# RWKV-7 attention and a four-expert mixture in one kernel: raw R loaded first, raw loads begun ahead of the x placement, later order of work from the seventh unit on

## The chip, the cores and the metric

The kernel runs on one core of one Trainium2 chip. The metric is the device time of one execution in microseconds (us). Before the change it is 1277.89 us, the median of 3 runs that lie between 1271.62 and 1294.58 us. The profiled execution took 1285.56 us, and its span from first to last instruction is 1283.8 us.

The engines are named as the profile names them: PE is TensorE (PEld its weight loads), DVE is VectorE, ACT is ScalarE, POOL is GpSimd, SP is SyncE, which here only issues transfers.

## The reference, cut to what matters

Two blocks follow each other. The first is a recurrence over 768 tokens, for 4 batches of 8 heads with 40 channels:

```python
for t in range(S):
    y[:, :, t] = np.einsum('bhd,bhde->bhe', rt, state)
    Sa = np.einsum('bhde,bhe->bhd', state, at)
    state = state * wt[:, :, None, :] - np.einsum('bhd,bhe->bhde', Sa, bt) \
            + np.einsum('bhd,bhe->bhde', vt, kt)
```

Its output, 3072 tokens by 320 channels, is the input x of the second block, a mixture of four experts with 1024 hidden channels each:

```python
for e in range(E):
    h = np.maximum(x @ w1[e], 0.0)
    out += p[:, e:e + 1] * (h @ w2[e])
```

Everything is float32.

## The kernel before, in words

**Units.** The recurrence is cut into chunks of 64 tokens. A *unit* is one chunk of two batches, so that its 128 tokens fill the partitions; there are 24 units. All units of one pair of batches hang together through `state`; two successive units belong to different pairs.

**The work of one unit.** It is spread over three generators, and the main loop (L1016 on) advances those of three successive units in turns.

- `within` (L385) is what needs no state. It turns the decays W into running products G and their reciprocals rG, brings B, A, K, V, R into channel order (tiles NT, AT, KT, VT, RT, by `turn_raw`, a DVE transpose at L229), multiplies three of them by rG or G (L423), and then runs small matmuls on PE: `pc` (L374) from RT and VT, `pfe` from NT, AT and KT, `pev`.
- `substitute` (L521) inverts small triangular blocks. DVE prepares M (L526 to L545: copies, the transpose L529, then L541 and L545), and POOL runs a serial chain of 48 small products and sums on tile Z (L554, L567).
- `merge` (L573) starts with two DVE transposes, Qc out of Z (L578) and QTc out of Qc (L580), goes on with `pY` and `pQ` on PE and fills QT.
- `step` (L613) brings in the state: `prn`, `psat`, `pxr`, `pdy` on PE, SX, Y and the new state on DVE, and at its end it places Y into the tile xT of the mixture. From the third chunk on this placement is 12 transfers (L718), which wait for Y.

**The mixture.** For each chunk of both pairs of batches (256 tokens) `mixture_of_chunk` (L822) puts 16 pieces of work on a list: per expert two `up` halves (ph, L733 and L741, read by ACT as hs, L746), and two pieces `down_1` (product p431) and `down_2` (products p75 and p26), which belong to the expert before. `down_2` comes with `add_h`, five DVE additions a1, a7, a5, a2, a6 of 512 columns (L842). DVE also adds the products onto the output tiles osb (L757, L759). `mix` takes pieces off the list and emits them between the stages of the recurrence; a regular unit emits 8, that is two experts: up, p431, up, p75 and p26, and the same again.

The PSUM buffers of `ph` and of the products share one tag, `mm`, with three buffers, so an `up` can only start when DVE or ACT has read what lay in its two buffers.

**Transfers.** SP issues nearly all of them in one queue, in the order of the program. Each of the six raw tiles (`rawW`, `rawA`, `rawB`, `rawK`, `rawV`, `rawR`) has one buffer, and is loaded by four transfers (six for W). The loads of unit u+3 but for W are put on a list `later`, and `begin_later` issues some of them behind every piece of the mixture; the weights w1 come in pieces of 640 KB through two buffers (L288).

**The order of the instructions.** The program is recorded in the order of the main loop. Instructions under `keep_in_program_order` keep that order among themselves, such as Qc, QTc, M and the transfers of `later`. All others are set by a scheduler that estimates when their inputs are there. On the chip each engine works through its own list in the order so found. From the unit with index 3 on (`q.u > PADDED`), the instructions of `within` are not kept in order, so the places of NT, AT, KT, VT, RT and of `pc` in their queues are the scheduler's.

**The main loop.** A flag `early` (L1036) decides where in unit u the stages of `merge` and `step` of unit u+1 stand: for early units the first stage of `merge` (Qc, QTc) comes in the third part of the loop, for later units in the second part, ahead of the pieces of the mixture there. It is set for u below 5.

Of the kernel before, what the change touches and what calls it, by code (L numbers as in the profile page):

```python
# [15 lines left out]
def kernel(  # L16
# [159 lines left out]
    units = []  # L176

    def begin(u):
        q = Unit()
        q.u, q.c, q.bp = u, u // (B // 2), u % (B // 2)  # L180
        q.b = [2 * q.bp, 2 * q.bp + 1]
        q.start, q.end = q.c == 0, q.c == NC - 1
        q.n = {}
        units.append(q)
        return q

    def load(q, names):
        for x in names:
            q.n[x] = t = sb.tile([P, H, D], FP32, name=f"nat{x}", tag=f"nat{x}", bufs=2 if x == "V" else 1)
            for i, bb in enumerate(q.b):  # L190
                nc.sync.dma_start(
                    out=t[i * L:(i + 1) * L], in_=srcs[x][bb, :, q.c * L:(q.c + 1) * L, :].rearrange("h t e -> t h e"),
                )

    def load_raw(q, names):


        moves = []
        for x in names:
            q.n["raw" + x] = t = raw[x]()  # L200
            heads = srcs[x].rearrange("b h t e -> (b h) t e")[q.b[0] * H:(q.b[1] + 1) * H, q.c * L:(q.c + 1) * L, :]
            heads = heads.rearrange("n (x two) e -> x n (two e)", two=2)
            for r in range(2):
                hs = slice(r, 16, 2)
                for y, los, w_ in ((0, (0,), D + Q), (1, (0, D) if x == "W" else (0,), D - Q if x == "W" else 2 * D - Q)):
                    o = slice(64 * r + Q * y, 64 * r + Q * y + Q)
                    for lo in los:
                        cols = slice(Q * y + lo, Q * y + lo + w_)
                        moves.append(
                            lambda eng, out=t[o, :, lo:lo + w_], in_=heads[:, hs, cols]: eng.dma_start(out=out, in_=in_)  # L210
                        )
        return moves
# [10 lines left out]
    def go(moves, eng=None):  # L223
        for move in moves:
            move(eng or nc.sync)
# [347 lines left out]
    def merge(q):  # L573


        Qc = sb.tile([P, H, Q], FP32, name="Qc", tag="q", bufs=2)
        QTc = sb.tile([P, H, Q], FP32, name="QTc", tag="q", bufs=2)
        tc.keep_in_program_order(nc.vector.transpose(out=dealt(Qc[:]), in_=q.Z))  # L578
        tc.keep_in_program_order(
            nc.vector.transpose(  # L580
                out=QTc[:].rearrange("p h r -> p (h r)"), in_=Qc[:].rearrange("p h c -> p (h c)"),
            )
        )
        q.QT = QTs()
        for i in range(P // Q):
            ins = nc.gpsimd.tensor_copy(out=q.QT[quarter(i), :, quarter(i % 2)], in_=QTc[quarter(i)])  # L586
            tc.keep_in_program_order(ins)
        yield

        py = big("pY")  # L590
        for h in range(H):
            for i in (1, 3):
                nc.tensor.matmul(
                    out=py[quarter(i - 1), h * Q:(h + 1) * Q], lhsT=q.F[quarter(i), h, 0:Q],
                    rhs=QTc[quarter(i), h, :], start=True, stop=True,
                )
        Y = sb.tile([P, H, Q], FP32, name="Yq")
        for i in (0, 2):
            nc.scalar.copy(out=Y[quarter(i)].rearrange("p h t -> p (h t)"), in_=py[quarter(i), 0:H * Q])
        yield  # L600

        pq = big("pQ")
        for h in range(H):
            for i in (0, 2):
                nc.tensor.matmul(  # L605
                    out=pq[quarter(i), h * Q:(h + 1) * Q], lhsT=Qc[quarter(i), h, :],
                    rhs=Y[quarter(i), h, :], start=True, stop=True,
                )
        for i in (0, 2):
            nc.scalar.copy(out=q.QT[quarter(i), :, quarter(1)], in_=by(pq[quarter(i), 0:H * Q], Q))  # L610
        yield
# [157 lines left out]
    def mixture_of_unit(q):  # L769

        hs, at = {}, 2 * E * q.u

        def ups(e):
            hs[e] = [up(at + 2 * e + x, q.xT, P, P) for x in range(2)]
            used(at + 2 * e + 2)
            if q.u == 0 and e + 2 < E:
                load_w2(e + 2)

        def down(e):
            po = ps.tile([P, DM], FP32, name="po", tag="mm", bufs=3)  # L780
            for f in range(NF):
                nc.tensor.matmul(  # L782
                    out=po[:], lhsT=hs[e][f // HF][:, f % HF, 0:P], rhs=w2_sb[e][:, f, :],
                    start=(f == 0), stop=(f == NF - 1),
                )
            if e == 0:
                q.osb = outputs()
            add(q.osb[:], po[:], scale(q, e), e == 0)
            if e == E - 1:
                store(q, q.osb)  # L790

        todo.append(lambda: ups(0))
        for e in range(E):
            todo.append(lambda e=e: down(e))
            if e + 1 < E:
                todo.append(lambda e=e: ups(e + 1))
# [111 lines left out]
    todo, last, later = [], [], []  # L908

    def begin_later(n):  # L910
        for move in later[:n]:
            tc.keep_in_program_order(move(nc.sync))
        del later[:n]

    def mix(n):

        for piece in todo[:n]:
            piece()
            begin_later(3 if n > 1 else 6)
        del todo[:n]  # L920

    def run(gen, n=99):
        if gen is None:
            return
        for _ in range(n):
            if next(gen, gen) is gen:
                break
# [3 lines left out]
    def begin_step(u):  # L931
        q = units[u]
        if q.bp == 0:
            chunks_x[q.c] = sb.tile([P, 3, 2 * P], FP32, name="xT", tag="xT", bufs=2)
        q.xT = chunks_x[q.c][:, :, q.bp * P:(q.bp + 1) * P]
        return step(q, q.xT)
# [57 lines left out]
    load(units[3], "BKV")  # L994
    go(load_raw(units[3], "ABKVR"))
    mix(3)
    m, s = merge(units[1]), begin_step(1)
    run(m, 1)
    mix(1)
    run(m)  # L1000
    run(s, 2)
    run(ws[2], 2)
    mix(1)
    run(ws[2], 2)
    substitute(units[2], nc.gpsimd)
# [10 lines left out]
    for u in range(1, NU):  # L1016
        q = units[u]
        m = s_next = w = w_next = iter(())
        if u + 1 < NU:
            m, s_next = merge(units[u + 1]), begin_step(u + 1)  # L1020
            w_next = ws[u + 1]
        if u + 2 < NU:
            w = ws[u + 2]

        def gap(n, pieces=None):
            at = 4 * u + n
            run(sum_ops, sums_at.get(at, 0))
            mix((1 if at in sparse else 2) if pieces is None else pieces)

        run(w, 1)  # L1030
        run(w_next)
        run(s, 1)
        gap(0)


        early = u < 5  # L1036
        run(s, 1)
        run(w, 1)
        run(s)
        if u == 1:  # L1040
            mixture_of_unit(q)
        elif q.bp:
            mixture_of_chunk(units[u - 1:u + 1], chunks_x[q.c])
        begin_later(len(later))
        run(w, 1)
        if not early:
            run(m, 1)
        gap(1)

        if u + 3 < NU:  # L1050
            go(load_raw(begin(u + 3), "W"))
            load(units[u + 3], "BKV")
            later.extend(load_raw(units[u + 3], "BAKVR"))
        run(w, 1)
        if early:
            run(m, 1)
        else:
            run(s_next, 1)
            run(m, 1)
        gap(2)  # L1060

        if not early:
            run(m, 1)
        run(w, 1)
        if not early:
            run(s_next, 1)
        if u + 2 < NU:
            substitute(units[u + 2], nc.gpsimd)
        run(w, 1)
        if u + 3 < NU:  # L1070
            ws.append(within(units[u + 3]))
            run(ws[u + 3], 1)
        if early:
            run(m, 1)
            run(s_next, 1)
            run(m)
            gap(3, 1)
            run(s_next, 1)
            mix(0 if 4 * u + 3 in sparse else 1)
        else:  # L1080
            gap(3)
        s = s_next
# [31 lines left out]
```

## Time and profile before

| what | measured |
|---|---|
| time, median of 3 | 1277.89 us |
| span of the profile | 1283.8 us |
| PE busy | 1200.6 us, 94% |
| DVE busy | 829.7 us, 65% |
| POOL busy | 475.2 us, 37% |
| ACT busy | 331.1 us, 26% |
| mean granted TensorE clock | 0.887 |
| moved through HBM | 94 GB/s over the span |

The page gives, under 2, the busy share of each engine in 40 equal slices, and the clock that PE was granted in each of them:

```profile
PE   5889988999999999999989999999999999999998
...
DVE  7865576789656756676566666676666766644334
POOL 4024555464253351552524515425244253350000
PEclk7789987999797887997979899789797997899999
```

Each digit is a tenth. PE is busy nearly throughout, and the recurrence ends some 150 us before the end, where POOL falls to 0 and only the mixture is left. The row PEclk is to be read beside the row PE: where it shows 7 or 8, PE was busy and yet worked on a reduced clock for part of the slice. A line of the groups reads: source line, engine, operation, tiles written and read, shapes, count, then the busy time in us and the mean ns of one, then the idle time just before and what ended it.

### The profile page before, as it was taken

The page shows a single profiled execution, that of the slowest core. Times are in us where ns is not written, and L with a number is a line of the kernel's source. Part 1 is how long each engine was busy: PE and PEld are TensorE (multiplying, and loading weights), DVE is VectorE, ACT ScalarE, POOL GpSimd, SP SyncE. Part 2 cuts the span into 40 slices and gives each one's busy share as a digit, 9 for nine tenths or more (in the row PEclk, how much of TensorE's full clock was granted, in tenths as well). Part 3 has the DMA queues.
Part 4 walks back from the last instruction along what each step waited for, and adds up shares of the span by engine and source line. Part 5 has one row for each costly group of instructions (what it writes and reads, how often), then busy time and mean ns, then how long its engine had stood idle before and what let it go on. Part 6 is the DMA issues. An engine that isn't in the chain of part 4 may idle for free.

```text
span 1283.8 us, 38036 instructions
## 1 busy us (share of the span) xinstructions
PE 1200.6 (94%) x15828; PEld 1045.6 (81%) x15828; DVE 829.7 (65%) x1642; ACT 331.1 (26%) x844; POOL 475.2 (37%) x1226
## 2 busy tenths in 40 slices
PE   5889988999999999999989999999999999999998
PEld 4767766888788888888878888888888887888887
DVE  7865576789656756676566666676666766644334
ACT  2222333223223122232231322322213323122110
POOL 4024555464253351552524515425244253350000
PEclk7789987999797887997979899789797997899999
DMA  7657642445334424443343443442434334212221
GB/s 147 141 135 196 137 91 67 98 101 125 84 99 100 105 74 99 95 114 85 84 109 85 108 104 87 104 99 72 107 86 112 86 104 89 84 57 86 86 76 31
DMA packets 299491, 126.73 MB, mean 99 GB/s; under 512 B 244360, under 2 KB 272696, under 8 KB 299320
## 3 DMA queue, kind: packets, MB, share of 16 engines
q1 hardware_dynamic: 296312, 123.84, 40.5%
q8 instruction: 125, 2.05, 0.7%
q10 hardware_dynamic: 3008, 0.46, 0.2%
q14 instruction: 46, 0.38, 0.1%
HBM read 116.36 MB, written 3.93 MB: 94 GB/s over the span
## 4 chain that ended last, share of the span: by engine, by line
PE 75%; DVE 10%; SPq 7%; DMA 5%; issue 2%; ACT 1%; DVEq 0%; ACTq 0%
PE ph L741 25%; PE p L848 20%; PE ph L733 9%; SPq L718 3%; PE pfe L374 3%; PE pdy L374 2%; PE psat L374 2%; PE prn L374 2%; DMA w1p<-in_moe_w_dram 2%; PE po L782 2%; SPq L210 2%; PE pxr L374 2%; PE pQ L605 2%; DVE osb L759 2%; PE pc L374 1%
## 5 line engine op out<-in xcount | busy, mean ns | idle before, releaser
L741 PE MATMUL ph<-xT,w1p 128*128 128x256 f32 (+1 forms) x1520 | 370.1, 400 | 0.0
L741 PEld LDWEIGHTS ph<-xT,w1p 128*128 128x128 f32 x1520 | 293.3, 203 | 74.6 <-issue 26.3
L567 POOL TENSOR_TENSOR Z<-Z 128x31 f32<-128x31 f32 (+7 forms) x704 | 256.9, 365 | 55.2
L554 POOL TENSOR_TENSOR Z<-M,Z 128x62 f32<-128x62 f32 (+7 forms) x352 | 156.0, 443 | 294.9 <-DVE M L545 258.6
L842 DVE TENSOR_TENSOR a<-hs 128x512 f32<-128x512 f32 x220 | 152.5, 710 | 145.6 <-ACT hs L746 145.6
L746 ACT ACTIVATE hs<-ph 128x512 f32<-128x512 f32 (+1 forms) x208 | 117.2, 564 | 439.9 <-PE ph L741 439.6
L759 DVE SCALAR_TENSOR_TENSOR osb<-p,gate,osb 128x320 f32<-128x320 f32 (+1 forms) x243 | 108.1, 480 | 128.6 <-PE p L848 125.1
L848 PE MATMUL p<-sums,a 128*128 128x160 f32 x1056 | 164.8, 299 | 0.0
L586 POOL COPY QT<-QTc 32x256 f32<-32x256 f32 x96 | 40.1, 418 | 326.7 <-DVE QTc L580 309.1
L848 PEld LDWEIGHTS p<-sums,a 128*128 128x128 f32 x1056 | 152.9, 190 | 2.2
L733 PE MATMUL ph<-xT,w1p 64*128 64x256 f32 (+1 forms) x760 | 138.1, 442 | 0.6 <-ACT xT L710 0.6
L848 PE MATMUL p<-w,hs 128*128 128x160 f32 x704 | 104.2, 301 | 0.0
L848 PE MATMUL p<-w,a 128*128 128x160 f32 x704 | 102.8, 299 | 0.0
L848 PEld LDWEIGHTS p<-w,hs 128*128 128x128 f32 x704 | 100.8, 191 | 2.3
L848 PEld LDWEIGHTS p<-w,a 128*128 128x128 f32 x704 | 98.0, 190 | 0.0
L733 PEld LDWEIGHTS ph<-xT,w1p 64*128 64x128 f32 x760 | 79.5, 207 | 20.1 <-issue 6.3
L439 DVE RECIPROCAL rG<-G 128x504 f32<-128x504 f32 x24 | 79.1, 3296 | 0.0
L634 ACT COPY SN<-prn 64x256 f32<-64x256 f32 x88 | 32.2, 366 | 159.0 <-DVE EV L630 156.6
L529 DVE STREAM_TRANSPOSE M<-blocks 128x1024 f32<-128x1024 f32 x24 | 46.3, 1931 | 35.4 <-ACT blocks L526 35.1
L374 PE MATMUL pc<-RT,VT 40*64 40x64 f32 x768 | 21.2, 264 | 40.4 <-DVE RT L229 39.0
L374 PEld LDWEIGHTS pc<-RT,VT 40*64 40x64 f32 x768 | 17.3, 168 | 46.7 <-DVE RT L229 43.6
L374 PE MATMUL pdy<-VC,k_tok 64*64 64x104 f32 (+1 forms) x768 | 43.6, 269 | 0.0
(153 smaller groups left out, 1489.7 us busy)
## 6 DMA issues: line engine op xcount, KB each, us to landing
w1p<-in_moe_w_dram SPq DMA_DIRECT2D x95, 512.0 KB
w1p<-in_moe_w_dram SPq DMA_DIRECT2D x190, 64.0 KB
w<-in_moe_w_dram SPq DMA_DIRECT2D x4, 1280.0 KB
sums<-in_moe_w_dram SPq DMA_DIRECT2D x9, 512.0 KB
out_dram<-osb SPq DMA_DIRECT2D x46, 80.0 KB
rawW<-in_w_dram SPq DMA_DIRECT2D x47, 72.0 KB
natB<-in_b_dram SPq DMA_DIRECT2D x42, 80.0 KB
natK<-in_k_dram SPq DMA_DIRECT2D x42, 80.0 KB
```

The lines of the kernel that those rows point to most:

```text
L374: nc.tensor.matmul(out=p[row][half(col), lo + at * out_cols:lo + (at + 1) * out_cols], lhsT=lhsT, rhs=rhs, start=(n == 0), stop=(n == len( ...
L439: pin(nc.vector.reciprocal(out=rG[:, :, 0:L - 1], in_=Gv[:, :, 1:L]))
L529: ins = nc.vector.transpose(out=M[:], in_=cols)
L554: ins = eng.tensor_tensor(out=Z[:, 1:3, 0:n, j + 1:Q], in0=M[:, j:j + 2, None, j + 1:Q].to_broadcast([P, 2, n, m]), in1=Z[:, here, 0:n, j: ...
L567: eng.tensor_tensor(out=z[:, 0], in0=z[:, 0], in1=z[:, x], op=ALU.add)
L586: ins = nc.gpsimd.tensor_copy(out=q.QT[quarter(i), :, quarter(i % 2)], in_=QTc[quarter(i)])
L733: nc.tensor.matmul(out=ph[i][:, f, :], lhsT=w1.last[i * DT:(i + 1) * DT, f, :], rhs=xT[i * DT:(i + 1) * DT, 2, :], start=(f == 0), stop=False,
L741: nc.tensor.matmul(out=ph[i][:, f, :], lhsT=w1.main[:, g, at * P:(at + 1) * P], rhs=xT[:, g, :], start=False, stop=(g == 1 and f == HF // ...
L746: nc.scalar.activation(out=h[:, i * HF // 2:(i + 1) * HF // 2, 0:n], in_=ph[i][:], func=ACTF.Relu,)
L759: nc.vector.scalar_tensor_tensor(out=to, in0=p, scalar=sc, in1=to, op0=ALU.mult, op1=ALU.add)
L842: nc.vector.tensor_tensor(out=t[:], in0=x, in1=y, op=op)
L848: nc.tensor.matmul(out=p[:, n * HD:(n + 1) * HD], lhsT=a[:, f, :], rhs=b[:, f, :], start=(f == 0), stop=(f == HF - 1),)
```

## The change

It has four parts.

1. The list `later` is filled in the order R, B, A, K, V instead of B, A, K, V, R.
2. Behind each piece of the mixture four raw transfers are issued instead of three, where `mix` has more than one piece to emit.
3. What is left of the list is issued ahead of the last stages of `step`, and so ahead of the 12 transfers of the placement. It stood behind them before.
4. The flag `early` holds for u below 6 instead of 5, so the later order of the loop begins at the seventh unit.

It is meant to have RT in time for `pc`, and to keep raw loads from standing behind transfers that wait for Y.

```diff
@@ def mix(n)
         for piece in todo[:n]:
             piece()
-            begin_later(3 if n > 1 else 6)
+            begin_later(4 if n > 1 else 6)
@@ for u in range(1, NU)
-        early = u < 5
+        early = u < 6
         run(s, 1)
         run(w, 1)
+        begin_later(len(later))
         run(s)
         if u == 1:
             mixture_of_unit(q)
         elif q.bp:
             mixture_of_chunk(units[u - 1:u + 1], chunks_x[q.c])
-        begin_later(len(later))
         run(w, 1)
@@
             load(units[u + 3], "BKV")
-            later.extend(load_raw(units[u + 3], "BAKVR"))
+            later.extend(load_raw(units[u + 3], "RBAKV"))
```

## The prediction

> **What bounds the kernel now.** The page gives PE 94% busy, so I asked for PE's waits first. One row stands out:
>
> ```profile
> PE pc L374 <- DVE RT L229: 39.0, 18, 3.2
> ```
>
> Columns: total us, times, longest. From 334 us on it is 16 times the same 2.16 us, once a unit. The timeline of PE, then of DVE, around two of them, and SP and POOL between:
>
> ```profile
> 490.29 1.25 PE L848 MATMUL p<-sums,a 128*128 128x160 f32 x8
> 493.70 0.69 PE L374 MATMUL pc<-RT,VT 40*64 40x64 f32 x32 [2.16 <-DVE RT L229]
> ```
>
> ```profile
> 485.21 2.35 SPq L210 DMA_DIRECT2D rawR<-in_r_dram  x2
> ```
>
> ```profile
> 439.88 0.58 DVE L578 STREAM_TRANSPOSE Qc<-Z 128x256 f32<-128x256 f32 x1
> ...
> 456.71 0.69 DVE L545 TENSOR_TENSOR M<-M,Z 128x512 f32<-128x512 f32 x1
> ...
> 492.64 0.38 DVE L759 SCALAR_TENSOR_TENSOR osb<-p,minus_gate,osb 128x160 f32<-128x160 f32 x1
> 492.94 0.70 DVE L229 STREAM_TRANSPOSE RT<-rawR 128x512 f32<-128x512 f32 x1
> 493.56 0.58 DVE L578 STREAM_TRANSPOSE Qc<-Z 128x256 f32<-128x256 f32 x1
> ```
>
> ```profile
> 457.55 0.29 POOL L554 TENSOR_TENSOR Z<-M,Z 128x62 f32<-128x62 f32 x1 [14.30 <-DVE M L545]
> ...
> 479.66 0.51 POOL L567 TENSOR_TENSOR Z<-Z 128x8 f32<-128x8 f32 x2
> 494.76 1.29 POOL L586 COPY QT<-QTc 32x256 f32<-32x256 f32 x3 [14.58 <-DVE QTc L580]
> ```
>
> The raw R was asked for at 485-487.6, and RT ran at 492.94 directly behind osb additions: the wait is the DVE queue, not a late transfer. The second thing to see is POOL: from M (457.40) to the end of the chain (480.2) it needs 22.7 us, and Qc, which reads its result, stands in DVE's queue only at 493.56, 13 us later. This chain costs nothing today.
>
> The windows show what the wait does beyond its 2.16 us (PE, PEld, DVE, ACT, POOL busy, then the granted clock):
>
> ```profile
> 438.00:440.00 2.00, 0.00 (x0) 0.00 (x0) 2.00 (x5) 0.00 (x0) 0.00 (x0) 1.00 0.34 49
> ...
> 442.00:444.00 2.00, 2.00 (x66) 1.82 (x62) 1.06 (x4) 0.73 (x2) 1.15 (x3) 0.50 0.68 118
> ...
> 458.00:460.00 2.00, 2.00 (x16) 1.97 (x15) 0.00 (x0) 0.60 (x1) 1.56 (x6) 1.00 0.10 23
> ```
>
> ```profile
> 440.01:493.70 53.69, 51.53 (x661) 44.94 (x661) 34.48 (x68) 13.71 (x35) 20.90 (x53) 0.84 0.38 90
> 493.70:545.76 52.06, 49.90 (x660) 43.56 (x660) 34.66 (x68) 13.71 (x35) 20.54 (x53) 0.87 0.42 99
> 545.76:593.71 47.95, 45.43 (x661) 40.39 (x661) 34.55 (x68) 13.71 (x35) 21.07 (x53) 0.96 0.43 102
> ```
>
> After each wait the clock is halved, for 17.1, 13.7 or 3.4 us. Units of equal work take 53.7, 52.1 and 47.95 us accordingly, 52.1 on average (334.33 to 1115.52 is 15 units). Taking the wait and the rest of the halving out leaves 47.95 - 2.16 - 1.4 = 44.4 us.
>
> **What the Trainium skill says.** "Perfetto Trace Analysis", section Tensor Engine Instruction, says ACT, DVE and GpSimd are strict FIFO: a waiting DVE instruction holds all behind it. The trace agrees: RT, with its data there, waited for its place. "TensorE: Matmul & The Clock Gate", Part 1, says an idle window of about 3.4 us puts PE on half clock, a busy one restores it. The lengths found are multiples of 3.4 us, but here 2.16 us idle was enough, and the measurement decides. "GPSIMD Engine Reference", section 1, says POOL shares its SBUF interface with DVE: L554 on 128x152 ranges up to 1006 ns, beside a median of 398 for the line, and the chain took 20.25 us at 90-110 us, 21.5 in the last unit, 22.7 otherwise.
>
> **The change part by part.** No operation is added or removed; every count stays.
>
> Loads (R first, four behind a piece, the rest ahead of the placement): SP issues the same transfers. The two rawR transfers behind the placement (2.35 us) move ahead of it, where SP stood waiting for Y (472.5 to 476.26). PE has no waits on w1p rows, so this is worth 0 by itself.
>
> What it moves is the scheduled order, and that I read from the built programs, for index 8 on. On PE `pc` moves ahead of p75 and p26, or between them. On DVE, RT moves from the end of the unit to right behind SX, and Qc, which in both programs follows RT closely, moves with it. Before, 45 DVE instructions stand between M (L545) and the Qc that reads its chain. After, in 10 units only 7 to 14 (adds of p431, SX, RT, then Qc: "near"), and in 6 units 21 (also a1, a7, a5, a2 and p75's adds: "far"). The POOL order is unchanged. So DVE will reach Qc long before POOL is done and stand there, with additions, Y, AT, KT, VT queued behind. PE soon follows: its third `up` needs the PSUM buffer that p75's adds free (near), or p431 the one p26's adds free (far). A loop forms that was hidden: M, POOL chain, Qc, the DVE and PE work to the next M.
>
> Its length I walk at full clock. Durations are from the rows of the unit at 440-494: up 4.6 us (474.43 to 479.05), p431 3.35 (to 482.40), up 4.6 (to 487.03), p75 with p26 4.4; DVE and ACT rows are the ones shown in the same timeline (a 0.68, an add of 320 columns 0.5, of 160 columns 0.3).
>
> - Near. Qc 0.58, QTc 0.45, a1 and a7 1.36, p75's adds and a5 1.5: the third up may start 3.9 us after Qc began. PE then does up 4.6, p431 3.35, up 4.6 and p75 2.2, so pc comes at 18.7. VT is there by then (DVE has some 14 us of work, and one a1 that waits for the last up). Then pc 0.55, prn 1.0, pY 0.55, p26 2.2, pQ 0.55, pfe 0.95, psat 0.9: 25.4. ACT's SaT, SX and blocks (2.65; 451.07 to 453.63) have to pass before DVE's transpose L529: 28.1. L529 to L545 take 3.4: M is ready 31.6 after Qc.
> - Far. p75's adds stand ahead of Qc, so PE is held only at p431, until p26's adds and a6 are done: 2.1. p431 and up end at 10.1. But VT comes behind QTc 0.45, NT 0.65, Y and state 3.7, rG on NT 0.7, AT 1.35, four adds 1.6, KT 1.35 and its own 0.65, together 10.4 of DVE: 12.5. So pc at 12.6 with a wait of 2.4 before it; then the same small products with p75 and p26, 8.9; ACT 2.65; and DVE has the 3.3 us reciprocal (L439) between L529 and L545. M is ready 31.3 after Qc.
>
> To both comes POOL's chain. With DVE mostly idle beside it, it is unknown between the shortest seen, 20.25, and the usual 22.7; I take 20.5 (near) and 21 (far), since the two short ones were those with the least DVE work beside them. With 0.15 from M to POOL the loops are 52.3 and 52.4 us.
>
> The idle PE costs clock as well. Ahead of a near Qc, PE runs out of work at 42.5 (far loop: psat 21.5, up, p431, 1.5 for pev and pxr, up, 4.4, 2.5 for pdy and pg) and is freed at 52.4 + 3.9: nearly 14 us idle. Ahead of a far Qc it runs out at 50.9 and is freed at about 54.5: some 4 us. Both exceed 2.16 us, so the clock halves every time. Dense up work then needs one or two windows of 3.4 us to restore it: 3.4 to 6.8 us at half speed, on average a loss of 2.5 us, which I add to the near loop; in the far loop VT's 12.5 hides it. Near 54.8, far 52.4.
>
> Sum: from the first early Qc (index 8) to the last (23) are 10 near and 5 far loops: 810 us, now 1115.38 - 387.82 = 727.6. That is +82. The first comes earlier: M at about 345 (now 351.73) plus 20.5 is 366 instead of 387.8: -22. Behind the last Qc are now 168.4 us; after, pc follows at 12.6, and from pc on 168.3, less 5.5 us of halved clock, plus 4.4 for p75 and p26: 179.8, +11. In all +72: 1350 us.
>
> `early` below 6 concerns one unit, whose Qc stays behind pc; taken as 0 beside the 6 us above.
>
> **The rivals.**
>
> - The wait goes and the clock stays full: 15 units at 44.4 instead of 52.1, and 7 in the last: -123, 1155 us. For it: RT and VT stand early enough for pc. Against: POOL's 22.7 us after M would have to fit ahead of Qc; it overruns by over 10.
> - DVE stalls, but the halved clock falls on idle time: 785 us of loops, 1325.
> - Nothing measurable: a chain below 19 us and more PE overlap give loops of 50, 750 us: 1290. Against: no chain below 20 in the trace.
> - Worse: chain at 22.7 and two more windows at half clock, near 59.5, far 56.7: 879 us, 1419.
>
> **How the numbers follow.** Forecast 0.50, milder stall 0.24, worse 0.12, faster 0.07, nothing measurable 0.07. The range 1305 to 1400 takes in forecast, the milder stall and the lower half of the worse case. Faster 0.07, same 0.08, slower 0.85.
>
> **What would show it.** Right: DVE waits on POOL Z at L578, 8 to 15 us each, 16 times; PE waits of several us at ph L733 and p L848 on DVE osb; the row pc <- RT gone; loops from Qc to Qc of 52 to 55 us; POOL chains nearer 20 than 22.7. Wrong: no such DVE wait, or PE going on while DVE stands, which would need PSUM buffers free that I count as taken.

## Result and the profile after

The changed kernel takes 1340.42 us (median of 3 runs, 1337.48 to 1342.32) against 1277.89. The ratio is 1.0512, with a 95% interval from 1.0436 to 1.0589: slower by some 5%. This ratio and those of the experiments leave slow runs out (here the one of 1294.58 us), and the experiments are compared with runs of the kernel before made beside them (medians 1282.63 and 1284.18 us), so the ratios differ a little from the quotients with 1277.89.

PE's waits after, with the columns as before (total us, times, longest). The row `pc <- RT` is gone, and PE now stands before `up`, with a smaller new wait of `pg` for rG:

```profile
PE ph L733 <- issue: 106.0, 11, 12.3
PE pg L341 <- DVE rG L440: 23.9, 8, 4.0
...
PE pc L374 <- DVE VT L229: 7.9, 3, 3.7
```

"issue" says only that the view saw no releaser. DVE's waits give the reason. The row of Qc before, then after:

```profile
DVE Qc L578 <- POOL Z L567: 3.5, 1, 3.5
```

```profile
DVE Qc L578 <- POOL Z L567: 162.8, 17, 16.7
```

Before, Qc waited once, in the last unit. Now it waits for POOL's chain 17 times. One of these waits, on DVE, POOL and PE, in the timelines (start us, duration us, engine, line, operation, then the idle time before it in brackets):

```profile
647.05 0.69 DVE L545 TENSOR_TENSOR M<-M,Z 128x512 f32<-128x512 f32 x1
647.66 1.59 DVE L759 SCALAR_TENSOR_TENSOR osb<-p,gate,osb 128x320 f32<-128x320 f32 x4
649.16 0.77 DVE L381 COPY_PREDICATED SX<-mask_up,pxr 128x256 f32<-128x256 int32 x2
649.82 0.71 DVE L229 STREAM_TRANSPOSE RT<-rawR 128x512 f32<-128x512 f32 x1
666.95 0.61 DVE L578 STREAM_TRANSPOSE Qc<-Z 128x256 f32<-128x256 f32 x1 [16.42 <-POOL Z L567]
```

```profile
647.89 0.29 POOL L554 TENSOR_TENSOR Z<-M,Z 128x62 f32<-128x62 f32 x1 [28.05 <-DVE M L545]
...
666.40 0.51 POOL L567 TENSOR_TENSOR Z<-Z 128x8 f32<-128x8 f32 x2
```

```profile
648.30 3.72 PE L741 MATMUL ph<-xT,w1p 128*128 128x256 f32 x16
...
658.63 0.70 PE L733 MATMUL ph<-xT,w1p 64*128 64x256 f32 x2
671.06 2.04 PE L733 MATMUL ph<-xT,w1p 64*128 64x256 f32 x6 [11.74 <-issue]
673.04 5.03 PE L741 MATMUL ph<-xT,w1p 128*128 128x256 f32 x16
```

RT runs right behind SX, and Qc is next in DVE's queue, 16.4 us before POOL is done (666.91). All of DVE's work stands behind it, among it the osb additions that free PSUM. PE runs dry at 659.3 and starts again 4.1 us after Qc. The last line shows what the idle time costs on top: the same 16 matmuls that took 3.72 us at full clock take 5.03.

Where the 56.6 us between the two spans (1283.8 and 1340.4) lie, cut at the start of the first Qc that moved ahead and of the last one before the last unit (the 8th and the 23rd):

| stretch | before | after | difference |
|---|---|---|---|
| start to the 8th Qc | 334.2 | 327.0 | -7.2 |
| 8th to 23rd Qc, 15 loops | 781.2 | 834.1 | +52.9 |
| 23rd Qc to the end | 168.4 | 179.3 | +10.9 |

### The profile page after: what moved, and what is told of

It is laid out like the page before. It is cut to its first block, busy times and chain, and to the rows that moved or that the text cites. A ratio compares the mean times of both kernels' runs of the same rounds, so it can differ in the third digit from the quotient of the medians.

```text
span 1340.4 us, 37990 instructions
## 1 busy us (share of the span) xinstructions
PE 1152.9 (86%) x15828; PEld 1001.3 (75%) x15828; DVE 818.2 (61%) x1642; ACT 330.8 (25%) x844; POOL 451.8 (34%) x1226
## 4 chain that ended last, share of the span: by engine, by line
PE 62%; DVE 15%; issue 8%; POOL 5%; DMA 3%; SPq 3%; ACT 3%; DVEq 0%; ACTq 0%; POOLq 0%
PE ph L741 22%; PE p L848 18%; PE ph L733 7%; POOL Z L567 3%; PE pdy L374 3%; PE po L782 3%; DVE rG L439 2%; SPq L718 2%; POOL Z L554 2%; DVE M L529 2%; DMA w1p<-in_moe_w_dram 2%; DVE osb L759 2%; PE psat L374 1%; PE pfe L374 1%; DVE G L402 1%
## 5 line engine op out<-in xcount | busy, mean ns | idle before, releaser
L554 POOL TENSOR_TENSOR Z<-M,Z 128x62 f32<-128x62 f32 (+7 forms) x352 | 138.4, 393 | 555.6 <-DVE M L545 446.7
L567 POOL TENSOR_TENSOR Z<-Z 128x31 f32<-128x31 f32 (+7 forms) x704 | 235.1, 334 | 55.2
L733 PE MATMUL ph<-xT,w1p 64*128 64x256 f32 (+1 forms) x760 | 131.1, 444 | 106.6 <-issue 106.0
L733 PEld LDWEIGHTS ph<-xT,w1p 64*128 64x128 f32 x760 | 77.9, 210 | 129.3 <-issue 117.3
L848 PE MATMUL p<-sums,a 128*128 128x160 f32 x1056 | 165.7, 300 | 0.0
L848 PEld LDWEIGHTS p<-sums,a 128*128 128x128 f32 x1056 | 152.2, 190 | 2.1
L578 DVE STREAM_TRANSPOSE Qc<-Z 128x256 f32<-128x256 f32 x24 | 14.8, 618 | 162.8 <-POOL Z L567 162.8
L848 PE MATMUL p<-w,hs 128*128 128x160 f32 x704 | 104.7, 302 | 0.0
L848 PE MATMUL p<-w,a 128*128 128x160 f32 x704 | 104.7, 300 | 0.0
L848 PEld LDWEIGHTS p<-w,hs 128*128 128x128 f32 x704 | 101.4, 192 | 2.2
L586 POOL COPY QT<-QTc 32x256 f32<-32x256 f32 x96 | 52.6, 548 | 147.7 <-DVE QTc L580 142.6
L848 PEld LDWEIGHTS p<-w,a 128*128 128x128 f32 x704 | 98.2, 190 | 0.3
L374 PE MATMUL pdy<-VC,k_tok 64*64 64x104 f32 (+1 forms) x768 | 48.0, 274 | 0.0
L374 PE MATMUL pdy<-SX,n_tok 64*64 64x104 f32 (+1 forms) x768 | 46.3, 264 | 0.4 <-DVE SX L381 0.4
```

The costliest lines, as they stand in the source:

```text
L374: nc.tensor.matmul(out=p[row][half(col), lo + at * out_cols:lo + (at + 1) * out_cols], lhsT=lhsT, rhs=rhs, start=(n == 0), stop=(n == len( ...
L554: ins = eng.tensor_tensor(out=Z[:, 1:3, 0:n, j + 1:Q], in0=M[:, j:j + 2, None, j + 1:Q].to_broadcast([P, 2, n, m]), in1=Z[:, here, 0:n, j: ...
L567: eng.tensor_tensor(out=z[:, 0], in0=z[:, 0], in1=z[:, x], op=ALU.add)
L733: nc.tensor.matmul(out=ph[i][:, f, :], lhsT=w1.last[i * DT:(i + 1) * DT, f, :], rhs=xT[i * DT:(i + 1) * DT, 2, :], start=(f == 0), stop=False,
L848: nc.tensor.matmul(out=p[:, n * HD:(n + 1) * HD], lhsT=a[:, f, :], rhs=b[:, f, :], start=(f == 0), stop=(f == HF - 1),)
```

## The experiments

Two theories. **Stall:** R first lets RT float up to SX, and Qc goes with it (its instruction is tied behind the one recorded just before it on DVE, which is RT; in the trace after, Qc follows RT directly or 4 instructions later in every unit from the 8th to the 23rd), so DVE waits for POOL; without that the change would have gained, since it takes away the wait of `pc`. **Transfers:** the raw loads, issued earlier, set the time by when they land or by what they collide with.

### Each part alone

R first, nothing else:

```diff
-            later.extend(load_raw(units[u + 3], "BAKVR"))
+            later.extend(load_raw(units[u + 3], "RBAKV"))
```

> The kernel before with only the order of the raw loads changed (R, B, A, K, V); three behind a piece, the rest behind the placement, early below 5. In its built DVE order 7 instructions stand between M and Qc in 16 units. Stall theory (R first moves RT, and Qc behind it, so that DVE stands at Qc for POOL): all loops are of the near kind, 57 us, so 16 waits of DVE on POOL Z of 12 to 17 us and a time of 1340 to 1390 us, no better than the full change. Transfer theory (what costs is the larger share of raw loads issued early, ahead of w1 pieces and placement, and R first is harmless): within 2% of the kernel before, 1255 to 1300 us.

Measured: 1448.83 us, ratio 1.1236 (1.1147 to 1.1325). Its waits of PE and of DVE:

```profile
PE ph L733 <- issue: 132.7, 18, 11.0
PE pc L374 <- DVE VT L229: 39.6, 18, 3.2
```

```profile
DVE Qc L578 <- POOL Z L567: 236.2, 18, 16.5
```

The direction is that of the stall, and the size goes beyond what was expected of it. The second row gives a reason: here `pc` still stands behind p26 in PE's queue and now waits for VT, the last of the five, 39.6 us in place of the 39.0 for RT. The old wait was kept and the stall added, in every unit from the 7th to the 23rd, with Qc 7 or 8 instructions behind M, near, from the 8th on. The loops are 60.6 us on average, (1249.1 - 339.4)/15, where 57 was expected.

The other three parts without R first:

```diff
-            begin_later(3 if n > 1 else 6)
+            begin_later(4 if n > 1 else 6)
...
-        early = u < 5
+        early = u < 6
...
+        begin_later(len(later))
         run(s)
...
-        begin_later(len(later))
```

> The changed kernel with the raw loads in the old order B, A, K, V, R; the other three parts stay. Qc stands 33 to 44 DVE instructions behind M. Stall theory: no wait at Qc of more than 2 us, pc already ahead of p75 and p26 on PE and so without its 2.16 us wait in most units; units of 45 to 49 us, time 1165 to 1230 us. Transfer theory: the loss stays, 1320 to 1350 us. A third view, that the later order of work costs: 1300 to 1350 us.

Measured: 1203.09 us, ratio 0.9351 (0.9295 to 0.9408). The wait of `pc` fell to 6.1 us, and Qc waits for POOL twice, 7.5 us in all. So one line of the change turns a gain of 6.5% into a loss of 5.1%. Which of the three brings the gain, the next three runs tell, each with one of these hunks alone.

> Of the change only part 2 is done: four raw transfers behind a piece of the mixture instead of three. In the built program pc then stands behind the second up or behind p75 and no longer behind p26, RT stands behind VT and ahead of the osb additions of p26, and 31 to 44 DVE instructions lie between M and Qc, so Qc has POOL's chain done when it is reached. Theory (the wait before pc and the clock that it halves are what before loses; DVE's stall at Qc is what the change loses): the pc <- RT row falls from 39 us to below 10, no wait on POOL Z at Qc, time 1190 to 1225. Rival (the gain of the version with all parts but R comes from the raw loads ahead of the placement or from the later order): 1260 to 1295, as before.

Measured: 1212.96 us, ratio 0.9444 (0.9383 to 0.9505).

> Of the change only part 3 is done: what is left of the raw loads is issued ahead of the placement. In the built program pc stays behind p26 as before; in every second unit RT stands behind a6 and all additions of osb, in the others as before; 41 to 52 DVE instructions lie between M and Qc. Theory (a load that starts earlier is worth nothing where the wait is DVE's queue): the pc <- RT row keeps its size, 30 to 45 us, no stall at Qc, time 1255 to 1300. Rival (the wait before pc is a late transfer of raw R, as the edit's purpose says): the row falls below 10 us and the time to 1190 to 1225.

Measured: 1279.88 us, ratio 1.0023 (0.9997 to 1.0049).

> Of the change only part 4 is done: the later order of the loop begins one unit later. In the built program only the units around it differ, from index 10 on 45 DVE instructions lie between M and Qc and RT is behind the additions of p26, as before. Theory (it concerns one unit): 1265 to 1290, pc <- RT at 35 to 45 us. Rival (it sets the order of all later units and so carries the gain): below 1230.

Measured: 1280.61 us, ratio 0.9963 (0.9922 to 1.0004).

The row of `pc` in the waits of these three, in the same order:

```profile
PE pc L374 <- DVE RT L229: 6.1, 2, 3.2
```

```profile
PE pc L374 <- DVE RT L229: 48.4, 17, 3.7
```

```profile
PE pc L374 <- DVE RT L229: 36.8, 17, 3.2
```

Four transfers behind each piece is the part that gains, and it gains by order: `pc` moves ahead of p26, and RT ahead of the additions that waited for it. Raw loads ahead of the placement, the part meant to have R there in time, leave the row at 48.4 us. No trace lists a wait of RT for its transfer either. This refutes the late transfer as the cause of the wait before `pc`: it was DVE's queue. That the loads ahead of the placement leave the time as it was hides a trade, more idle time at a higher clock: `pQ` waits 25.2 us for ACT there, where it was 2.2, and the mean clock is 0.902 in place of 0.887.

### Qc moved back, all else kept

In the changed kernel RT is recorded ahead of VT, so that Qc is tied behind VT. PE's order and that of the transfers on SP stay as in the changed kernel from first to last; DVE's differs (`PADDED` is 3; the kernel keeps the order of `within` for `q.u <= PADDED`, so its places are the scheduler's from the unit with index 4 on, not 3):

```diff
+            if q.u >= PADDED:
+                q.RT = by_channels("RT", "RT", 2, "R")
             VT = by_channels("VT", "turned", 3, "V")
-            q.RT = by_channels("RT", "RT", 2, "R")
+            if q.u < PADDED:
+                q.RT = by_channels("RT", "RT", 2, "R")
```

> The changed kernel with all four parts; only RT and VT are recorded in the other order, R before V, so that Qc is kept behind VT instead of behind RT. PE's order stays that of the changed kernel. Stall theory: waits at Qc fall from 163 us to under 25 us, the PE waits at ph go with them, units of 45 to 49 us, time 1165 to 1230 us. If the loss comes from RT or the loads instead: 1320 to 1350 us.

Measured: 1201.63 us, ratio 0.9339 (0.9266 to 0.9412), with every load where the change has it. DVE waits at Qc twice, and PE before `up` (L736 in this kernel) twice, 2.1 us in all. DVE's row, and what stays of PE's rows above:

```profile
DVE Qc L581 <- POOL Z L570: 6.0, 2, 5.2
```

```profile
PE pg L341 <- DVE rG L443: 23.5, 7, 4.0
...
PE pc L374 <- DVE VT L229: 6.9, 2, 3.7
```

This is the decisive run. The kernels of 1340 and of 1202 us issue the same transfers and the same matmuls in the same order; the place of Qc, 0.6 us, and of what is tied to it in DVE's queue makes the difference of 139 us. It also beats both kernels.

### Half the chain

The changed kernel with the second half of POOL's substitution left out (8 of its 16 steps are done):

```diff
-        for j in range(0, Q, 2):
+        for j in range(0, Q if at_once else Q // 2, 2):
```

> The changed kernel with the second half of POOL's chain left out (8 of the 16 steps of the substitution on POOL, so the inverted blocks are incomplete); order of DVE and PE as in the changed kernel. Stall theory: the chain takes 9 to 11 us instead of 19 to 21, each near loop falls by about 10 us until PE's 44 to 46 us of work hold, time 1180 to 1230 us, waits at Qc still there but under 8 us each. If POOL's chain isn't what holds the loop: within 2% of the changed kernel, 1315 to 1365 us.

Measured: 1233.02 us, ratio 0.9595 (0.953 to 0.9661). DVE's row:

```profile
DVE Qc L578 <- POOL Z L567: 56.1, 9, 7.1
```

A chain of 9.8 us in place of 19.2 gives back 107 us of the changed kernel's 1340, and the wait of a near Qc falls from 16.4 to 7.1, by as much as the chain is shorter. POOL's chain is thus what DVE waits for. The gain is shared out otherwise than expected: the loops behind a near Qc fell from 57.7 to 52.1 us and not by 10, those behind a far Qc from 51.3 to 43.4, since from the 13th Qc on the chain that a near Qc waits for runs in these. Even the half is too long for the near place, and the version with the whole chain and Qc behind VT is faster than this one.

### How long an idle time halves the clock

The kernel with Qc behind VT keeps 7 waits of `pg` of up to 4.0 us: it needs the reciprocal of 8 columns (0.20 us), which stood behind four additions (1.5 us) that stood behind the reciprocal of 504 columns (3.3 us). The order of the two is turned and the long one tied behind the short:

```diff
-        pin(nc.vector.reciprocal(out=rG[:, :, 0:L - 1], in_=Gv[:, :, 1:L]))
         pin(nc.vector.reciprocal(out=rG[:, :, L - 1:L], in_=q.gl[:]))
+        pin(nc.vector.reciprocal(out=rG[:, :, 0:L - 1], in_=Gv[:, :, 1:L]), True)
```

> The changed kernel with RT recorded ahead of VT, as in the run of that edit, and in addition the reciprocal of 8 columns (0.2 us) recorded ahead of that of 504 columns (3.3 us), which is pinned behind it. In that earlier run pg waited 7 times for the small reciprocal, which stood behind four additions of osb (1.5 us): 23.5 us in all, up to 4.0 us each, and the clock was halved for 3.4 to 6.8 us behind each. Theory (the idle time itself halves the clock, and 2.2 us are enough): the waits shrink to some 2.5 us each, 15 to 18 us in all, the clock is still halved behind each, and the time falls by 5 to 12 us from 1202 only, 1188 to 1200. Rival (only an idle time near 3.4 us or more halves the clock): behind waits of 2.5 us the clock stays full, and the time falls by 20 to 30 us, 1170 to 1185. Second rival (these waits are hidden): 1200 to 1206.

Measured: 1200.68 us, ratio 0.9354 (0.9296 to 0.9412). That cannot be told from 0.9339 without it; the row fell to 16.3 us and a new one, pdy behind SX, has 7.1. The time lies at the edge of the second rival's range, and as a way to gain time the edit failed. For the clock it is worth more, because one wait became far shorter than the others. Two of its waits on PE's timeline, and windows behind them (the columns end with clock, DMA share, GB/s):

```profile
538.70 0.93 PE L341 MATMUL pg<-ident,rG 128*128 128x128 f32 x4 [2.65 <-DVE rG L443]
```

```profile
820.83 0.63 PE L341 MATMUL pg<-ident,rG 128*128 128x128 f32 x4 [0.85 <-DVE rG L443]
```

```profile
540.00:543.00 3.00, 2.63 (x11) 1.56 (x11) 0.64 (x2) 1.47 (x4) 2.53 (x7) 0.50 0.06 11
...
821.50:824.50 3.00, 2.00 (x13) 1.45 (x14) 1.27 (x5) 1.47 (x4) 2.45 (x8) 1.00 0.26 49
```

The first window lies behind the wait of 2.65 us and has half the clock; behind 0.85 us the clock stays full. All five waits of 2.59 to 2.67 us from 536 us on were followed by 3.4 to 6.8 us of halved clock, the one of 0.85 us by none. Behind three of the five, though, a second wait of 1.0 us (`pdy`) came before the clock fell; only two, at 538.70 and 634.34, stand alone, beside the 16 of 2.16 us in the kernel before. So an idle time well below 3.4 us can be enough, and the expectation that only one near 3.4 us does it is refuted.

The length of one wait does not decide it, though. In the run with R first alone, `pc` waits 2.16 us in 16 units, and behind 5 of these waits the clock stays full. Two of the 16 end at 426.91 and 488.66 us. The windows around each (behind the span stands PE's busy time):

```profile
423.51:426.92 3.41, 1.25 (x11) 1.01 (x10) 3.22 (x7) 0.00 (x0) 0.00 (x0) 1.00 0.49 72
426.92:430.34 3.42, 3.42 (x120) 3.30 (x122) 1.31 (x5) 0.18 (x1) 0.00 (x0) 0.50 0.74 123
```

```profile
484.95:488.36 3.41, 1.55 (x12) 1.31 (x10) 3.28 (x7) 0.00 (x0) 0.00 (x0) 1.00 0.75 206
488.36:491.78 3.42, 3.12 (x134) 2.75 (x134) 2.40 (x8) 1.06 (x3) 0.00 (x0) 1.00 0.51 79
```

These windows are not cut at the waits. In every trace here the changes of the clock between 60 and 1190 us fall on one grid of 3.413 us (worked out from the clock in windows of 0.25 us), and these are cells of it. The first wait lies within one cell, which has 3.41 - 1.25 = 2.16 us without PE work, and the next cell is halved. The second is split over two cells, 1.86 us and 0.30 us, and the next cell is not halved. Counted over all ten traces from 160 to 1190 us, every full-clock cell with 2.0 us or more without PE work was followed by a halved one. With 0.7 to 1.98 us both happened; what decides there stays open. A wait of 0.93 us was followed by a halved clock at 170 us in the kernel before, between small products, and another of the same length at 246 us was not.

## Why the prediction was right, step by step

**The wait before `pc` is DVE's queue, and goes.** Right: the row is gone (what is left is three waits for VT, 7.9 us), and the run with the raw loads ahead of the placement shows that a load issued earlier doesn't remove it.

**The loads are worth 0 by themselves.** Right for the placement (1.0023). Four behind a piece, which the prediction put under the same 0, gives 5.6% alone; but through the order that it makes the scheduler choose, which the prediction counted as moves.

**DVE reaches Qc too early, and PE soon follows.** Right for near Qc: PE was held at L733 (10 times, and the clock fell each time), freed 4.1 us after Qc began (3.9 predicted), idle 11.7 us in the unit shown (nearly 14). The ten near waits were 9.9 to 16.7 us, where 8 to 15 was written, 150.4 us of the row's 162.8. Wrong for far Qc: their waits were 0.4 to 3.5 us. DVE came late, and the predicted wait of PE at p L848 isn't there: in the far loop from 726.44 to 776.84 us PE has no listed wait.

**The loops.** Ten loops behind a near Qc took 57.7 us on average, where 54.8 was predicted, five behind a far Qc 51.3 (52.4). The parts:

| us | predicted | measured |
|---|---|---|
| near, Qc to M, with 2.5 for the clock | 34.1 | 37.0 |
| chain behind a near loop's M | 20.5 | 20.8 |
| far, Qc to M | 31.3 | 32.1 |
| chain behind a far loop's M | 21.0 | 19.2 |

(The far terms, as the prediction lists them, add to 30.9 and not 31.3.) The mis-sized term is Qc to M in a near unit. In the unit shown `pc` comes 21.2 us behind Qc (18.7 predicted, and the 2.5 for the clock explains that), but from `pc` to the end of `psat` it takes 10.3 us and not 6.7: waits of 0.8 us before pQ and 1.7 us within `psat`, and 1.08 us for pQ, taken as 0.55. Small products that wait on ACT and DVE in turn were walked as if PE were their only limit. Behind `psat` the 6.2 us of ACT and DVE came out as predicted.

**Clock.** The windows of a near and a far loop (after the span: PE, PEld, DVE, ACT, POOL busy, then the clock):

```profile
666.95:726.44 59.49, 50.54 (x666) 43.34 (x666) 37.40 (x73) 13.70 (x35) 21.30 (x53) 0.87 0.37 87
726.44:776.84 50.40, 42.78 (x658) 37.91 (x654) 30.28 (x61) 13.71 (x35) 17.78 (x53) 0.95 0.40 96
```

Over the whole span the changed kernel has the higher clock, 0.906 against 0.887: there is less halving, and much of what is left falls on idle time. From the 8th Qc on the clock is halved for 160 us, of which 75 lie in PE's listed waits; before it was 212 us, of which 2. A higher mean clock beside a longer time is no contradiction; PE is busy 86% of the span where it was 94%.

**The sum.** Predicted were -22, +82 and +11 us against the measured -7.2, +52.9 and +10.9. The tail was right. The other two hold a slip of counting: the first Qc that moves is the 8th, which began at 334.19 us before, and the prediction started from the 9th, at 387.82. It so compared 15 loops after with 14 before, and put the head one unit too late. From the right unit its own steps give M at 303.64 - 6.7 = 296.9 and Qc at 317.4, and 317.4 + 810 + 179.8 = 1307 us. The measured terms are 327.0, 834.1 and 179.3. The mechanism and the direction were right. That 1350 came so near 1340 is luck: the slip of some 43 us made up for loops and a head that were sized 33 us too short.

**The chances.** The case of a lost wait at full clock, put at 0.07 and 1155 us, points the way that the same change goes without R first (1203, at a mean clock of 0.950). The argument against it, that 22.7 us of POOL work would have to fit ahead of Qc, held for the order that R first brings and not for the other three parts.

## What to carry to other kernels

Ahead of a change in load order, ask which instructions the scheduler ties to the one that will move, and what they wait for; a transpose of 0.6 us that came along cost 139 us. A wait of 2 us behind an in-order queue can be paid twice, by itself and in the clock behind it (in the kernel before it was, 16 times of 16), so order can be worth more than its microseconds. When several edits come together, run each alone: here one part gained 5.6%, two were worth nothing, and one cost 12%.

## What was not expected of the hardware

- An idle time of 2.2 to 2.7 us on PE was mostly followed by a halved clock, for 3.4 to 17.1 us, but 5 of the 16 waits of 2.16 us with R first alone were not, where they were split over two cells of the grid of 3.41 us. From 2.0 us of idle time in one cell on, the clock was halved each time. The Trainium skill, "TensorE: Matmul & The Clock Gate", Part 1, speaks of an idle window of about 3.4 us; the length fits, but the window need not be idle throughout, and the measurement decides.
- POOL's chain of 48 operations took 19.2 us with DVE waiting beside it, 21.3 to 21.7 with DVE at work for most of it, and 22.5 to 22.9 in the 8th to the 23rd unit before (the 3rd to the 7th took 20.2 to 25.7, so the "22.7 otherwise" of the prediction doesn't hold for these; and its 1006 ns stood beside a median over all widths, where 128x152 alone took 450 to 460 ns in 14 of 22 cases). "GPSIMD Engine Reference", section 1, names the shared SBUF interface of the two; that this is the reason is argued here and not shown. From 19.2 to 22.9 us it is 19%.
